# Lagging one half of TensorE by three products in the tail of two attention layers, with earlier splits and stores

## The chip, the cores and the metric

The kernel runs on one core of a Trainium2 chip. Its engines work at the same time, each from its own queue in order: TensorE (PE, with its weight loads shown apart as PEld), VectorE (DVE), ScalarE (ACT), GpSimd (POOL) and SyncE (SP), which here issues nearly all DMAs. An engine that needs another's result waits on a semaphore, and all that is queued behind the waiting instruction waits with it. The metric is the device time of one execution in microseconds (us); the time given for a kernel is the median of several runs.

## The reference, cut to what matters

Two attention layers over 2048 positions, width 576, 32 heads of 18. Their outputs stand side by side.

```
A: qkv = x @ wqkv; each position attends to 8 positions at distances 0, 2, ..., 14
   behind it (masked before the start); softmax over the 8; heads joined; @ wo
B: qkv = x @ wqkv; scores of all 2048 x 2048 pairs of each head, scaled by 18 ** -0.5;
   softmax over the keys; weighted sum of the values; heads joined; @ wo
out = concat(A, B) along the last axis          # 2048 x 1152, float32
```

All inputs are float32. The kernel keeps that precision on TensorE by splitting a number into a high part in TensorE's rounded format (F32R) and the low rest, and adding the products high x high, high x low, low x high.

## The kernel before, in words

**Projections.** The first part computes all queries, keys and values of both layers and stores them in DRAM (`dqk`, `dv`, `da`).

**Layer B.** The heads are taken in eight groups of four (`g`), the queries in four blocks of 512 (`b`), the keys in sixteen tiles of 128 (`kt`). One triple of these is a step; there are 512, and steps 448 to 511 are the last group, g = 7, with its blocks starting at steps 448, 464, 480 and 496. A step computes four score tiles, one per head, on TensorE (`score`, L271): heads 0 and 2 in the upper 64 rows of the array, heads 1 and 3 in the lower 64. ACT makes the exponential of each (L279), and a step later TensorE multiplies them with the values into the bank `po` (`weigh`, L744), where a column of ones gives the denominators too.

The maximum to be subtracted is found beforehand, for groups ahead of the one being weighed: TensorE computes the scores once more (L160), VectorE reduces them (L168). When a block's maxima are complete, `least` reduces them (L178), a step later `turn` transposes them on VectorE (L185), a step later `halve` splits them on POOL into a high and a low part (L103, L104), and two steps later in the last group `place` writes them by eight small DMAs into spare rows of the query tile `qs` (L197). The scores of that block then come out with the maximum already subtracted, so the first `score` of a block waits for these eight DMAs. In the last group the lead of the maxima has shrunk to a few steps.

**Order.** All engines get their instructions in the order in which the Python code makes them. What isn't part of a step's fixed pattern stands in an agenda: `later(n, f)` and `plan(start, ...)` put a piece of work at a step, and `due()` makes it at the end of that step, in the order in which it was put down. What a finished block needs is such a chain: `finish` copies `po` to `o`, the denominators go through DRAM and come back spread out (`den`, `drec`, `rec`, L787 to L790), POOL multiplies (L791), splits the result (L792, L793) and it is stored to `do`. For block (7,0), `finish` runs in step 464 and L791 is due 13 steps later.

**Output products of B.** The rows of `wo` for B are loaded into the buffer `y` (L858) by `load_wo`, in steps 455, 457, 459 and 461 for the four large chunks, and split six steps later on POOL into the room of an old group's queries and keys. After block b of the last group is done, `full(b)` makes eight sums, one for each of four position tiles `t` and two halves `h` of 288 columns; `sum_of` makes one. It puts the contraction's upper 64 rows and lower 64 rows on the two halves of the array, in two banks, by `beside`, which issues an upper and a lower product in turn (L1137). There are 14 products in each half, or 12 for the sums of block 3 that are made without the last group (`partial`). ACT then copies the upper bank into `y` (L1161) and VectorE adds the lower one (L1162). These banks come from a ring of three (`else`); scores have a ring of four.

While maxima are still to be computed, sums are placed inside a step (`inside`). When none are left, the loop is in its paired form (`paired`): scores of an even step, a sum, scores of an odd step, a sum, the weighing of both steps (16 products), and where many sums wait a third one behind it. From here to the end I call it the tail.

**The end.** When the last block has been weighed, `closing` normalises it in pieces, `first` and `some` make the remaining products (L1108), and `end` stores the four position tiles of block 3 (L1188). The results stand in the buffer `y`, of which there are four; `full` stores a position tile through `later(1, ...)` (L1201).

**DMA.** SP issues its DMAs in order, and an issue that waits for data holds up those behind it.

Of the kernel before, what the change touches and what calls it, by code (L numbers as in the profile page):

```python
# [10 lines left out]
AF = mybir.ActivationFunctionType  # L11
# [6 lines left out]
D = 576  # L18
# [4 lines left out]
NG = H // 4  # L23
# [9 lines left out]
STEPS = NB * NT  # L33
# [28 lines left out]
def two_attentions(ctx: ExitStack, tc, xa, wa, woa, xb, wb, wob, out):  # L62
# [19 lines left out]
    def bank(kind=None):  # L82
        r = rings[kind or ring]
        r.append(r.pop(0))
        return p_bank.tile([128, 512], F32, name=f"bank{r[-1]}")
# [24 lines left out]
    def later(n, f):  # L110
        agenda[step + n].append(f)
# [37 lines left out]
    def block(g, b):  # L149

        qs, ks = sets[g % 3]

        mx = maxes.tile([128, 2, 2, 4, NB, 2], F32, name="mx", bufs=3)
        left = 2 * PIECES

        def take(ps, r, t, k, p, part=None):

            at = slice(64 * r, 64 * r + 54)
            first, n = (0, 512) if part is None else (256 * part, 256)
            return nc.tensor.matmul(ps if part is None else ps[:, 256 * r : 256 * r + 256],  # L160
                                    qs[at, b, p, 128 * t : 128 * t + 128],
                                    ks[at, p, 512 * k + first : 512 * k + first + n], start=True, stop=True)

        def reduce(ps, r, t, k, p, part=None):

            nonlocal left
            at = mx[:, r, p, t, k] if part is None else mx[:, :, p, t, k, part]
            nc.vector.tensor_reduce(at, ps.rearrange("q (s n) -> q s n", s=2), axis=AX.X, op=ALU.max)  # L168

            settle()  # L170
            left -= 1
            if left == 0:
                owing.append(least)

        def least():
            m = least_rooms[n_least[0] % 2]
            n_least[0] += 1
            nc.vector.tensor_reduce(m[:, :16], mx.rearrange("q r p t k s -> q (r p t) (k s)"), axis=AX.X, op=ALU.max,  # L178
                                    negate=True)
            later(1, lambda: turn(m))  # L180

        def turn(m):

            raw = maxes.tile([128, 32], F32, name="mt", bufs=2)
            nc.vector.transpose(raw, m)  # L185
            later(1, lambda: halve(raw))

        def halve(raw):
            mh = maxes.tile([128, 32], F32R, name="mh", bufs=2)
            split_on(nc.gpsimd, mh, raw.bitcast(F32R), raw)  # L190
            later(2 if g == NG - 1 else 5, lambda: place(mh, raw))

        def place(*parts):
            placed.add((g, b))
            for k, t in enumerate(parts):
                for j in range(4):
                    load(ap(qs.bitcast(F32)[54 + k : 128 : 64, b, 0, 32 * j :], (128, 8), (1, 32)),  # L197
                         t.bitcast(F32)[32 * j : 32 * j + 16])

        return take, reduce  # L200
# [922 lines left out]
    def beside(kind, *both):  # L1123

        sums_ = [bank(k)[:, :288] for k in (kind, None)]
        turns = [[(sums_[r], *ab, i == 0, i == len(t) - 1) for i, ab in enumerate(t)] for r, t in enumerate(both)]
        pair = kind and sum(given) + 2 <= NG * NB * PIECES * 2
        if pair:

            for r in range(2):  # L1130
                turns[r].insert(6 + 4 * r, None)
        for i in range(max(map(len, turns))):
            for r in range(2):
                if i < len(turns[r]):
                    if turns[r][i]:
                        ps, a, b, start, stop = turns[r][i]
                        nc.tensor.matmul(ps, a, b, start=start, stop=stop)  # L1137
                    else:
                        maximum(r)()
        if pair:  # L1140

            rings["else"].append(rings["else"].pop(0))
        return sums_

    def sum_of(y, t, h, chunks, kind=None, stack=()):

        pos, cols = slice(128 * t, 128 * t + 128), slice(288 * h, 288 * h + 288)
        both = []
        for r in range(2):
            both.append([])  # L1150
            for c, (hi, lo) in enumerate(chunks):
                at = slice(64 * r, min(64 * r + 64, hi.shape[0]))
                whi, wlo = wo["b"][c]
                both[r] += [(a[at, pos], w[at, cols]) for a, w in ((hi, whi), (hi, wlo), (lo, whi))]
            at = slice(64 * r, 64 * r + 3 * DH)
            both[r] += [(a[at, pos], w[at, cols]) for a, w in zip(stack, wstack)]
        one, two = beside(kind, *both)
        if kind:
            nc.vector.tensor_copy(y, one)
        else:  # L1160
            nc.scalar.activation(y, one, AF.Copy)  # L1161
        nc.vector.tensor_add(y, two, y)  # L1162

    def first(t, b, h):
        sums[t, b, h] = bank()[:, :288]
# [19 lines left out]
    def end(t, b, new):  # L1185
        for h in range(2):
            half_end(t, b, h, new)
        load(out[512 * b + 128 * t : 512 * b + 128 * t + 128, D:], ys[t, b])  # L1188

    def full(b):  # L1190
        def half(t, h):
            if total - sum(given) > 4:
                inside.append(lambda: quarter(t, h, "scores"))
            else:
                waiting.append(lambda: quarter(t, h))

        def quarter(t, h, kind=None):
            if h == 0:
                ys[t, b] = work.tile([128, D], F32, name="y", bufs=4)
            if h == 1:  # L1200
                later(1, lambda: load(out[512 * b + 128 * t : 512 * b + 128 * t + 128, D:], ys[t, b]))  # L1201
            sum_of(ys[t, b][:, 288 * h : 288 * h + 288], t, h, olds[b], kind, stacks[b])

        return [(4 + 2 * t + h, lambda t=t, h=h: half(t, h)) for t in range(4) for h in range(2)]

# [9 lines left out]

    for k, src, start, chunks in (
        ("a", woa, 28, [[(0, 128 * c, 128)] for c in range(4)] + [[(64 * r, 512, 64) for r in range(2)]]),
        ("b", wob, STEPS * (NG - 1) + 7,
         [[(0, 126 * c, 126)] for c in range(4)] + [[(32 * i, 504 + DH * i, DH) for i in range(4)]]),
    ):  # L1220
        plan(start, [((4 if k == "a" else 2) * c if len(ch) < 4 else 421 - start, lambda k=k, src=src, c=c, ch=ch: load_wo(k, src, c, *ch))
                     for c, ch in enumerate(chunks)])
# [69 lines left out]
    while step < ALL:  # L1292
# [18 lines left out]
        whole = total - sum(given) > 1  # L1311
        parts = (bool(begun) or total - sum(given) > 3) and step not in copied

        ps = bank() if inside and whole else None


# [20 lines left out]
        for _ in range(1 if paired and step < ALL - 2 else len(waiting)):  # L1337
            if waiting:
                waiting.pop(0)()
        if ready and (kt % 2 == 0 or not paired):  # L1340
            weigh(ready.pop(0))
        ready.append((g, b, kt, es))
# [32 lines left out]
```

## Time and profile before

| | |
|---|---|
| median of 3 runs | 1598.83 us (1594.93 to 1600.14) |
| profiled execution, its own time | 1596.11 us |
| its span, first to last instruction | 1594.3 us |
| granted TensorE clock | 1.0 |
| busy: TensorE, VectorE, ACT, POOL | 99%, 86%, 76%, 61% |

How it is read: busy shares are averages over stages with different limits. The chain that ended last goes back from the last instruction, at each step to what released it. In a timeline row stand the start, the duration, the engine, the line, the operation, output and inputs by their names in the program, the shape, the count, and in brackets the idle time of that engine just before, with what ended it. In a row of stretches stand the stretch, its length, the busy time of PE, PEld, DVE, ACT and POOL with their instructions, the clock, the share of the DMA engines and GB/s. Matmuls are pipelined and their ends are modelled, so rows overlap.

### The profile page before, as it was taken

What the parts mean: (1) busy time and instruction counts of PE and PEld (TensorE: products, weight loads), DVE (VectorE), ACT (ScalarE), POOL (GpSimd) and SP (SyncE); (2) the same over time, 40 slices, a digit from 0 to 9 for tenths busy, and PEclk for the clock granted to TensorE, in tenths of its full rate; (3) what the DMA queues carried; (4) which work ended last, traced back from release to release, by engine and by line L of the source; (5) the groups of instructions that cost most, each with busy time, mean ns of one, the idle gap of its engine ahead of it and who ended that gap; (6) DMA issues with size and microseconds to landing.
All of it is one profiled execution on the core that took longest, in us unless ns stands there. A gap on an engine that the chain in (4) does not pass through costs nothing.

```text
span 1594.3 us, 34958 instructions
## 1 busy us (share of the span) xinstructions
PE 1582.1 (99%) x13274; PEld 963.1 (60%) x13274; DVE 1369.1 (86%) x2313; ACT 1216.3 (76%) x2436; POOL 964.9 (61%) x798
## 2 busy tenths in 40 slices
PE   9999999999999999999999999999999999999998
PEld 7999888999644445445445445445445444545676
DVE  5299999999999999999989999999999999988622
ACT  6423441121699999999999999999999999998565
POOL 2405742211166996995896896896897898781000
PEclk9999999999999999999999999999999999999999
DMA  8938854532312352245226324422621331154311
GB/s 251 229 124 211 274 157 128 160 101 71 74 34 70 68 138 71 75 117 111 74 76 131 87 92 116 107 80 59 141 93 37 91 104 50 46 173 132 130 62 61
DMA packets 188025, 175.66 MB, mean 110 GB/s; under 512 B 119416, under 2 KB 133240, under 8 KB 186128
## 3 DMA queue, kind: packets, MB, share of 16 engines
q1 hardware_dynamic: 182992, 161.88, 36.7%
q0 software_dynamic: 4032, 10.63, 3.3%
q8 instruction: 104, 1.70, 0.5%
q10 hardware_dynamic: 832, 0.92, 0.2%
q14 instruction: 65, 0.53, 0.1%
HBM read 98.77 MB, written 73.47 MB: 108 GB/s over the span
## 4 chain that ended last, share of the span: by engine, by line
PE 94%; DVE 3%; POOL 1%; ACT 1%; issue 1%; DMA 0%; SPq 0%; POOLq 0%; DVEq 0%
PE po L744 30%; PE bank L271 19%; PE bank L160 17%; PE bank L366 16%; PE bank L303 5%; PE bank L1137 4%; PE bank L1264 4%; DVE mx L168 2%; POOL xlo L414 1%; PE bank L518 0%; ACT e L279 0%; SPq L197 0%; DMA out<-y 0%; DVE wlo L414 0%; DVE as L942 0%
## 5 line engine op out<-in xcount | busy, mean ns | idle before, releaser
L168 DVE TENSOR_REDUCE mx<-bank 128x2 f32<-128x512 f32 x2048 | 1278.8, 682 | 118.5 <-PE bank L160 89.1
L279 ACT ACTIVATE e<-bank 128x512 f32<-128x512 f32 x2048 | 1048.3, 606 | 62.3 <-PE bank L271 56.0
L160 PE MATMUL bank<-ks,qs 54*128 54x512 f32 (+1 forms) x2464 | 790.9, 381 | 2.1 <-DVE mx L168 1.2
L160 PEld LDWEIGHTS bank<-ks,qs 54*128 54x128 f32 x2464 | 403.0, 184 | 382.9 <-DVE mx L168 332.7
L271 PE MATMUL bank<-qs,ks 56*128 56x512 f32 x2048 | 592.5, 425 | 2.7 <-DMA qs<-mt 2.3
L744 PE MATMUL po<-e,v 128*19 128x512 f32 x4096 | 531.6, 599 | 0.1
L271 PEld LDWEIGHTS bank<-qs,ks 56*128 56x128 f32 x2048 | 308.8, 184 | 34.8 <-ACT e L279 25.1
L925 POOL TENSOR_TENSOR pr<-aq,akv 128x1024 f32<-128x1024 f32 x72 | 158.4, 2202 | 15.9 <-DMA akv<-da 13.0
L967 POOL TENSOR_TENSOR pr<-lg,akv 128x1024 f32<-128x1024 f32 x72 | 158.3, 2199 | 0.5
L744 PEld LDWEIGHTS po<-e,v 128*19 128x19 f32 x4096 | 73.7, 97 | 138.0 <-issue 132.1
L929 POOL TENSOR_TENSOR pr<-pr 128x1024 f32<-128x1024 f32 x64 | 152.7, 2386 | 5.0
L694 ACT ACTIVATE ohi<-bank 128x512 f32<-128x512 f32 (+1 forms) x56 | 30.4, 595 | 150.5 <-issue 107.7
L366 PE MATMUL bank<-xhi,ahi 64*128 64x512 f32 (+1 forms) x448 | 114.2, 387 | 0.0
L366 PE MATMUL bank<-xhi,alo 64*128 64x512 f32 (+1 forms) x448 | 112.1, 387 | 0.0
L366 PE MATMUL bank<-xlo,ahi 64*128 64x512 f32 (+1 forms) x448 | 111.1, 388 | 0.1
L1264 PE MATMUL bank<-wohi,at 64*128 64x288 f32 x480 | 103.2, 304 | 0.0
L968 POOL TENSOR_TENSOR pr<-pr 128x512 f32<-128x512 f32 x72 | 92.4, 1283 | 5.6
L1264 PEld LDWEIGHTS bank<-wohi,at 64*128 64x128 f32 x480 | 74.7, 184 | 27.6 <-ACT e L279 23.8
L414 POOL TENSOR_TENSOR alo<-raw,ahi 128x512 fp32r<-128x512 f32 (+1 forms) x14 | 17.6, 1255 | 121.6 <-ACT ahi L413 93.1
L506 POOL TENSOR_TENSOR olo<-olo,ohi 128x512 fp32r<-128x512 f32 x36 | 46.1, 1293 | 69.4 <-ACT ohi L505 59.4
L1264 PE MATMUL bank<-wolo,at 64*128 64x288 f32 x240 | 70.9, 295 | 0.0
L366 PEld LDWEIGHTS bank<-xhi,ahi 64*128 64x128 f32 (+1 forms) x448 | 64.8, 182 | 3.3
(200 smaller groups left out, 1795.6 us busy)
## 6 DMA issues: line engine op xcount, KB each, us to landing
do<-n SPq DMA_DIRECT2D x30, 512.0 KB
da<-ohi SPq DMA_DIRECT2D x52, 256.0 KB
akv<-da SPq DMA_DIRECT2D x64, 175.5 KB
out<-y SPq DMA_DIRECT2D x32, 288.0 KB
qs<-dqk SPq DMA_DIRECT2D x30, 288.0 KB
ks<-dqk SPq DMA_DIRECT2D x30, 288.0 KB
at<-dao SPq DMA_DIRECT2D x60, 128.0 KB
rec<-drec SPq DMA_DIRECT2D x29, 256.0 KB
```

Of the source, the lines that this page charges most:

```text
L160: return nc.tensor.matmul(ps if part is None else ps[:, 256 * r : 256 * r + 256], qs[at, b, p, 128 * t : 128 * t + 128], ks[at, p, 512 * k ...
L168: nc.vector.tensor_reduce(at, ps.rearrange("q (s n) -> q s n", s=2), axis=AX.X, op=ALU.max)
L271: nc.tensor.matmul(ps, ks[at, p, 128 * kt : 128 * kt + 128], qs[at, b, p], start=True, stop=True)
L279: nc.scalar.activation(e, ps, AF.Exp, scale=SCALE)
L303: nc.tensor.matmul(ps, a, b, start=c == i == 0, stop=c == 4 and i == 1)
L366: nc.tensor.matmul(ps, a, b, start=start, stop=stop)
L744: nc.tensor.matmul(po[32 * i : 32 * i + 19], vs[g][:, kt, 19 * i : 19 * i + 19], es[i], start=kt == 0, stop=kt == NT - 1)
L925: nc.gpsimd.tensor_mul(pr, ap(st["q"][:, 2 * c], (SUB, 2), (0, W), (1, SUB)), window(st["k"], c))
L929: nc.gpsimd.tensor_add(st["pr"], st["pr"], pr)
L967: nc.gpsimd.tensor_mul(at, ap(st["lg"], (0, 2), (SUB, W), (1, SUB)), window(st["v"], c))
L968: nc.gpsimd.tensor_add(at[:, :, :4], at[:, :, :4], at[:, :, 4:])
L1264: return nc.tensor.matmul(ps, a, b, start=r == k == 0, stop=r == 1 and k == len(both[1]) - 1)
```

## The change

There are five edits.

1. In `turn`, a block of the last group is split (`halve`) in the same step as it is transposed; `place` keeps its distance of two steps to the split.
2. `sum_of`, outside the `inside` form, no longer calls `beside`. It issues a product of the upper half, puts the matching one of the lower half into a queue `behind`, and issues from that queue until at most three are left in the paired form, none otherwise. So in the tail the lower half's last three products of one sum go beside the first three of the next, past scores and weighing. The upper bank is copied when the last upper product is issued, the lower one added when the last lower product is. The queue is emptied at the start of a step that has maxima or other inserted work, and in steps 510 and 511 after their sums.
3. `full` stores a position tile as soon as the addition of its second half is issued, no longer through the agenda one step later; the `inside` form still does.
4. `end` stores the last position tile (t = 3) in two halves of 288 columns, each as it is ready.
5. The four large weight chunks of B are loaded in steps 458 to 464 instead of 455 to 461; their splits move with them.

```diff
             nc.vector.transpose(raw, m)
-            later(1, lambda: halve(raw))
+            if g == NG - 1:
+                halve(raw)
+            else:
+                later(1, lambda: halve(raw))
...
-    def sum_of(y, t, h, chunks, kind=None, stack=()):
+    def sum_of(y, t, h, chunks, kind=None, stack=(), done=lambda: None):
...
-        one, two = beside(kind, *both)
         if kind:
+            one, two = beside(kind, *both)
             nc.vector.tensor_copy(y, one)
-        else:
-            nc.scalar.activation(y, one, AF.Copy)
-        nc.vector.tensor_add(y, two, y)
+            nc.vector.tensor_add(y, two, y)
+            done()
+            return
+        sums_ = [None, None]
+
+        def piece(r, i):
+            if i == 0:
+                sums_[r] = bank()[:, :288]
+            last = i == len(both[r]) - 1
+            nc.tensor.matmul(sums_[r], *both[r][i], start=i == 0, stop=last)
+            if last and r == 0:
+                nc.scalar.activation(y, sums_[0], AF.Copy)
+            elif last:
+                nc.vector.tensor_add(y, sums_[1], y)
+                done()
+
+        for i in range(len(both[0])):
+            piece(0, i)
+            behind.append(lambda i=i: piece(1, i))
+            catch_up(3 if paired else 0)
+
+    behind = deque()
+
+    def catch_up(n=0):
+
+        while len(behind) > n:
+            behind.popleft()()
...
     def end(t, b, new):
         for h in range(2):
             half_end(t, b, h, new)
-        load(out[512 * b + 128 * t : 512 * b + 128 * t + 128, D:], ys[t, b])
+            if t == 3:
+                load(out[512 * b + 128 * t : 512 * b + 128 * t + 128, D + 288 * h : D + 288 * h + 288],
+                     ys[t, b][:, 288 * h : 288 * h + 288])
+        if t < 3:
+            load(out[512 * b + 128 * t : 512 * b + 128 * t + 128, D:], ys[t, b])
...
-            if h == 1:
-                later(1, lambda: load(out[512 * b + 128 * t : 512 * b + 128 * t + 128, D:], ys[t, b]))
-            sum_of(ys[t, b][:, 288 * h : 288 * h + 288], t, h, olds[b], kind, stacks[b])
+            y = ys[t, b]
+
+            def done():
+                if h == 1:
+                    store = lambda: load(out[512 * b + 128 * t : 512 * b + 128 * t + 128, D:], y)
+                    later(1, store) if kind else store()
+
+            sum_of(y[:, 288 * h : 288 * h + 288], t, h, olds[b], kind, stacks[b], done)
...
-        ("b", wob, STEPS * (NG - 1) + 7,
+        ("b", wob, STEPS * (NG - 1) + 10,
...
+        if whole or parts or outside or inside:
+            catch_up()
         ps = bank() if inside and whole else None
...
         for _ in range(1 if paired and step < ALL - 2 else len(waiting)):
             if waiting:
                 waiting.pop(0)()
+        if step >= ALL - 2:
+            catch_up()
```

## The prediction

> **What bounds the kernel now.** I read the page first, then the chain that ended last, then, wherever the chain leaves TensorE, the timelines of the engines there.
>
> ```profile
> span 1594.3 us, 34958 instructions
> PE 1582.1 (99%) x13274; PEld 963.1 (60%) x13274; DVE 1369.1 (86%) x2313; ACT 1216.3 (76%) x2436; POOL 964.9 (61%) x798
> PE 94%; DVE 3%; POOL 1%; ACT 1%; issue 1%; DMA 0%; SPq 0%; POOLq 0%; DVEq 0%
> L168 DVE TENSOR_REDUCE mx<-bank 128x2 f32<-128x512 f32 x2048 | 1278.8, 682 | 118.5 <-PE bank L160 89.1
> ```
>
> TensorE is on 94% of the chain and VectorE's maxima fill most of the rest of the span. The change adds and removes no product, exponential or reduction; it moves waits. So only what TensorE waits for in the last group and after it can be won or lost: three places, A, B and D, and a row of small ones, C.
>
> **A. The maxima of block (7,2), split one step earlier.** TensorE's longest wait in the last group, with the chain into it (start, duration in us):
>
> ```profile
> 1462.37 0.47 PE L271 MATMUL bank<-qs,ks 56*128 56x512 f32 x1 [2.34 <-DMA qs<-mt]
> 1460.49 1.53 DMA qs<-mt
> 1456.42 2.30 SPq L197 DMA_DIRECT2D qs<-mh  x4
> 1458.82 2.17 SPq L197 DMA_DIRECT2D qs<-mt  x4
> 1451.25 0.20 DVE L185 STREAM_TRANSPOSE mt<-m 128x32 f32<-128x32 f32 x1
> 1454.96 1.29 POOL L791 TENSOR_TENSOR o<-o,rec 128x512 f32<-128x512 f32 x1 [17.99 <-DVE mx L168]
> 1456.19 0.20 POOL L103 CAST mh<-mt 128x32 fp32r<-128x32 f32 x1
> 1444.68 0.56 SPq L790 DMA_DIRECT2D rec<-drec  x1
> ```
>
> The transposed maxima are there at 1451.45, but their split (L103 and the subtraction after it) stands on POOL behind L791, which waits until 1454.96. The releaser named there, a reduction, is not what L791 reads; it reads rec, whose load was issued at 1444.68. In the code the turn of this block falls in step 476, the split in 477, and L791 is in 477 too, written into the agenda at step 464 and so ahead of it. Split in 476, it stands before L791. POOL has been idle for 17.99 us, so the split begins at 1451.45. The eight stores into the query rows follow 0.23 later (1456.42 - 1456.19), are issued over 4.07 (1460.49 - 1456.42) and land after 1.53: 1457.3, plus 0.35 from landing (1462.02) to product: 1457.6. TensorE came to the wait at 1462.37 - 2.34 = 1460.03. So the whole wait goes: -2.34. On SP the stores pass no DMA (the queue is empty from 1445.2 to 1456.4); POOL's L791 waits for rec either way and loses nothing. Late next is whatever step 480 needs; VectorE idles there too, for want of TensorE. Bounds: 0, if the stores land as slowly as those of block (7,1) in B, where the eight took 9.3 instead of 4.5; -2.34. I take -2.34, because the congestion ends by 1454.96, when rec is there.
>
> **B. B's output weights loaded three steps later.** Block (7,1) had the two first weight chunks ahead of it on SP; block (7,0) had not:
>
> ```profile
> 1408.26 1.80 SPq L858 DMA_DIRECT2D y<-wob  x2
> 1412.57 3.38 SPq L197 DMA_DIRECT2D qs<-mh  x4
> 1416.87 4.98 SPq L197 DMA_DIRECT2D qs<-mt  x4
> 1373.62 2.31 SPq L197 DMA_DIRECT2D qs<-mh  x4
> 1376.03 2.15 SPq L197 DMA_DIRECT2D qs<-mt  x4
> 1421.43 1.89 DVE L168 TENSOR_REDUCE mx<-bank 128x2 f32<-128x512 f32 x3 [0.16 <-PE bank L160]
> 1423.89 1.29 DVE L168 TENSOR_REDUCE mx<-bank 128x2 f32<-128x512 f32 x2 [0.58 <-PE bank L160]
> 1423.24 0.39 PE bank L271
> ```
>
> The eight stores stretch to 1421.85, and the first product of step 464 starts at 1423.24 instead of about 1422.8; VectorE idles 0.58 there against 0.16 a step before. That is 0.42 of stall. With chunks at steps 458 to 464 all eight stores go ahead of them: -0.42 (bounds 0 and -0.58). The chunks now pass, on SP, the store of n, drec, rec and the two stores of the A parts, or stand between them; on POOL their splits mix with L791 to L793 of block (6,3).
>
> ```profile
> 1435.01 0.91 SPq L997 DMA_DIRECT2D at<-dao  x2
> 1445.73 0.40 PE L1264 MATMUL bank<-wohi,at 64*128 64x288 f32 x1
> 1422.00:1426.00 4.00, 3.64 (x30) 1.20 (x22) 3.42 (x7) 3.52 (x8) 3.72 (x4) 1.00 0.79 228
> ```
>
> Two more chunks behind the stores are 2 x 290 KB, at the 228 GB/s of that stretch 2.5 us. The next loads TensorE needs are issued by 1435.9 and used at 1445.73, and POOL is idle for 18 us after this block: cost 0 (bounds 0 and +2.5, should everything behind shift into the use). The weights themselves are first used in step 486, by the code, 22 steps after the last of these loads.
>
> **C. The lower half three products behind.** A sum of output columns runs in two halves of the array, each into its own bank, out of three. In program order upper and lower products alternate before and after the change; only which lower product goes with which upper one differs. One sum that follows scores, with ACT beside it, and the sums as the chain shows them (first and last of the eight that follow the odd step's scores and hold 28 products; first and last of three that follow scores after the weighing, where nothing waits):
>
> ```profile
> 1558.52 0.59 PE L1137 MATMUL bank<-qs,wohi 64*128 64x288 f32 x2
> 1558.72 0.53 PE L1137 MATMUL bank<-ks,wohi 64*128 64x288 f32 x2
> 1556.23 2.07 ACT L279 ACTIVATE e<-bank 128x512 f32<-128x512 f32 x4 [2.02 <-PE bank L271]
> 1558.25 0.41 ACT L1161 ACTIVATE y<-bank 128x288 f32<-128x288 f32 x1
> 1516.38 2.04 PE bank L1137 x26
> 1572.79 2.03 PE bank L1137 x26
> 1556.36 1.85 PE bank L1137 x28
> 1570.33 1.86 PE bank L1137 x27
> 1504.21 2.16 PE bank L1137 x26
> 1549.21 2.01 PE bank L1137 x25
> 1522.81 1.90 PE bank L1137 x24
> ```
>
> The lower half's first product needs the bank that the sum before used above, and ACT copies it out only after four exponentials (1558.25 to 1558.66). The sum starts at 1558.52, its second products at 1558.72, just after the copy. Three products later, about 0.4 us, the copy is long done, so the wait goes: 2.04 - 1.85 = 0.19, eight times, 1.52. The first sum in the new order, at 1504.21, has the same wait (2.16 - 1.85 = 0.31) and that at 1549.21 too (2.01 - 1.85 = 0.16). The four sums of 24 products (1522.81 is one) are slow by some 0.27, 24 products being 24/28 of 1.85 = 1.59 and the row 1.90; I count them 0, because the scores behind them wait for ACT's fourth exponential, which does not come earlier. Paid once: before the last score step three lower products run alone, 3 x 0.13 = 0.40 (14 pairs in 1.85). Sum: 1.52 + 0.31 + 0.16 - 0.40 = 1.59 won. Bounds: 0.40 lost, if something else takes the place of every wait; 2.7 won, if the 24s give 0.27 each as well. I take -1.59, nearest to the rows of sums that wait for nothing.
>
> **D. The closing stores.**
>
> ```profile
> 1588.99 0.29 PE L1108 MATMUL bank<-qs,n 128*128 128x288 f32 x1
> 1587.42 2.48 DMA out<-y
> 1590.01 0.41 ACT L1181 ACTIVATE y<-bank 128x288 f32<-128x288 f32 x1 [2.78 <-DMA out<-y]
> 1590.03 0.46 DVE L1183 COPY y<-bank 128x288 f32<-128x288 f32 x1 [1.04 <-DMA out<-y]
> 1590.93 0.42 SPq L1201 DMA_DIRECT2D out<-y  x1
> ```
>
> The last product ends at 1589.28, but the last two copies wait until 1590.0 for a store to land: the first closing store, issued at 1587.42 and landed 2.48 later. Its buffer is taken again because one of the four y buffers is still held by the last sum of part C, whose store (L1201) the agenda issues only after the closing, last of all, at 1590.93. Issued at once, as changed, that store is away before the last scores are weighed and its buffer is free. The copies then start 0.7 earlier (1590.03 - 1589.32), the last store goes out at 1590.55 - 0.7 = 1589.85 instead of 1590.93: 1.08. It is also half as large, for which I take another 0.2 of its 2.48: -1.3. Bounds: -0.38 (only the queue place, 1590.93 - 1590.55, if the buffer is still waited for) and -1.5. One store more on SP costs 0.33 while SP waits for the copies: 0. By the Trainium skill, DMA: Bandwidth & Descriptors, section Anatomy of one DMA, about 2.0 us of a transfer are fixed, and by that half the bytes save little: -1.1. The row of 2.48 agrees with most being fixed; nothing else hangs on this.
>
> **Sum.** 2.34 + 0.42 + 1.59 + 1.3 = 5.65 us. The profiled execution took 1596.11 (span 1594.3 and 1.8 around it), so 1590.5 by its own time. It lies 2.7 below the median shown, 1598.83; from the median it is 1593.2, 0.35% less. A measurement of this kernel tells about 0.3%, 4.8 us, from no change.
>
> **The rivals.** R1: the placement of (7,2) is late in another way, its stores as slow as in B: 1451.7 + 9.3 of issue + 1.0 to land + 0.35 = 1462.4, as before, and 3.3 are left: 1595.5. Against it: rec has landed by 1454.96. R2: ACT sets the tail. Its four exponentials take 2.07 and the next scores need their banks, so the waits only change places; C becomes +0.40 and the sum 3.66: 1595.2. For it: the second copy of exponentials follows the copy without idle. Against: ACT idles 2.02 per pair of steps. By the Trainium skill, TensorE: Matmul & The Clock Gate, section on the array of 32x32 sub-arrays, ACT's queue is strictly in order; this favours R2, and the rows (copy behind exponentials) agree. R3: the change doesn't do what it says, the order of the agenda keeps L791 ahead and the stores late: 1598.8. R4, on the other side: a lower bank is now held over the weighing and given back only in the next sum, so VectorE's addition into y comes late, and the sum after it waits for that bank. It has 10 products and the scores, 1.3 + 0.47 us, and the addition takes 0.46:
>
> ```profile
> 1558.69 0.46 DVE L1162 TENSOR_TENSOR y<-bank,y 128x288 f32<-128x288 f32 x1 [4.00 <-PE bank L271]
> ```
>
> so it must be 1.3 us late to begin to cost, and 0.24 more on each of the 24 sums to eat the 5.65; at 0.6 on each it is +14.4 - 5.65: 1607.6. VectorE idles 4.00 ahead of such an addition, which speaks against it.
>
> **How the numbers follow.** Forecast 64%, R1 8%, R2 10%, R3 6%, R4 12%, more than its row bears, for losses in the order of instructions that a trace of before cannot show. The forecast's own range is 1589 to 1596.5: all upper bounds together are 2.34 + 0.58 + 2.7 + 1.5 = 7.1, and the runs spread by 2.6 about their middle. The range given, 1589 to 1598.3, takes in R1 and R2. Of the 64%, 53 lie beyond 4.8 us and 11 within; of R1 and R2 3 lie beyond. Faster 0.56, same 0.32, slower 0.12.
>
> **What would show it.** A: no wait of L271 on the query rows, and L103 ahead of L791 on POOL. B: eight stores in about 5 us, and no 0.58 on VectorE near step 464. C: the eight sums at 1.85, three lower products alone before the last scores. D: no wait of L1181 on a store; SP ends with half a y. Wrong would make it: a new wait of L271 or L1264 on a DMA between 1420 and 1480, or waits of L1137 on VectorE.

## The result, and the profile after

The changed kernel takes 1593.0 us (median of 15 runs, 1590.73 to 1594.35), the kernel before 1597.42 us (median of 15 runs on the same chips): the ratio is 0.9974, with a 95% interval of 0.9966 to 0.9982, so 2.9 to 5.4 us less. One execution of the kernel before took 2439.07 us, and the ratio is taken without it. The profiled execution took 1593.83 us. Some rows of the page of the changed kernel (line numbers after the change are higher by 3 to 40: `score` is L274, `weigh` L747, the tail's sums L1172, the closing copies L1208 and L1210):

```profile
span 1592.0 us, 34962 instructions
PE 1581.6 (99%) x13274; PEld 973.7 (61%) x13274; DVE 1371.2 (86%) x2313; ACT 1215.9 (76%) x2436; POOL 965.1 (61%) x798
L274 PE MATMUL bank<-qs,ks 56*128 56x512 f32 x2048 | 593.1, 425 | 0.0
```

The products are as many as before, and the score products (last row) no longer idle anywhere; before it was 2.7 us, 2.3 of them for a DMA. The span is only 2.3 us shorter than in the profile of before, 1592.0 against 1594.3, because this execution lost time elsewhere: the first exponential of layer B starts at 416.20 us, 2.45 later than in the profile of before (413.75). The projections ahead of it are the same code. Over the fourteen profiled executions of this study that start lies between 413.61 and 416.56, whatever was edited, so a span by itself cannot judge a change of 4 us here. What can is a table of stages. Each number runs from the start of one instruction to the start of another in the timeline: from the first exponential of step 448 to that of 464, and so on to step 511; from there to the last product; from the last product to the last copy into `y`; and from there to the end of the span.

| kernel | 448 to 464 | 464 to 480 | 480 to 496 | 496 to 511 | 511 to last product | to last copy | to the end | sum |
|---|---|---|---|---|---|---|---|---|
| before | 35.05 | 39.14 | 59.69 | 56.84 | 9.47 | 1.03 | 4.29 | 205.51 |
| changed | 34.65 | 36.74 | 59.32 | 56.01 | 9.59 | 0.33 | 4.12 | 200.75 |
| e1_split_late | 34.63 | 38.31 | 59.31 | 56.03 | 9.58 | 0.33 | 4.12 | 202.31 |
| e2_chunks_early | 34.65 | 36.74 | 59.26 | 56.01 | 9.60 | 0.33 | 4.35 | 200.93 |
| g11_neither | 34.68 | 37.74 | 59.22 | 55.98 | 9.60 | 0.33 | 4.13 | 201.67 |
| h12_again | 34.63 | 38.57 | 59.69 | 56.84 | 9.47 | 1.05 | 4.28 | 204.53 |
| e3_no_lag | 34.64 | 36.74 | 59.73 | 56.84 | 9.47 | 0.33 | 4.11 | 201.86 |
| f8_lag1 | 34.64 | 36.75 | 59.51 | 55.93 | 9.47 | 0.33 | 4.14 | 200.77 |
| f6_copy_dve | 34.65 | 36.74 | 59.28 | 55.98 | 9.58 | 0.33 | 3.99 | 200.55 |
| f7_dve_no_lag | 34.62 | 36.70 | 59.70 | 57.22 | 9.54 | 0.33 | 3.97 | 202.08 |
| e4_one_store | 34.64 | 36.70 | 59.30 | 56.01 | 9.58 | 0.33 | 3.75 | 200.32 |
| f5_store_late | 34.63 | 36.72 | 59.33 | 56.01 | 9.60 | 1.00 | 4.84 | 202.14 |
| g9_order | 34.64 | 36.74 | 58.74 | 55.44 | 9.59 | 0.33 | 3.96 | 199.43 |
| g10_all | 34.65 | 36.74 | 58.77 | 55.34 | 9.57 | 0.33 | 3.57 | 198.98 |

Where no transfer is waited for, a stage repeats to within some 0.1 us, so the table resolves what the medians cannot. The last stage holds the landing of a store: in the nine kernels that end with the same two half stores it lies between 3.96 and 4.35. Before against changed, the change won 0.40 and 2.40 in the two stages of B and A, 0.37 + 0.83 - 0.12 = 1.08 in C's three, and 0.70 + 0.17 = 0.87 in D's two: 4.76 in all, the 2.3 of the spans and the 2.45 lost ahead of layer B.

**A, around step 480.** POOL and then SP in the timeline of the changed kernel; in brackets the idle time before and what ended it:

```profile
1453.57 0.21 POOL L103 CAST mh<-mt 128x32 fp32r<-128x32 f32 x1 [13.18 <-DVE mt L185]
1456.38 1.29 POOL L794 TENSOR_TENSOR o<-o,rec 128x512 f32<-128x512 f32 x1 [2.27 <-DMA rec<-drec]
1453.80 2.30 SPq L200 DMA_DIRECT2D qs<-mh  x4
1456.20 2.17 SPq L200 DMA_DIRECT2D qs<-mt  x4
```

The split now starts as soon as the transposed maxima are there and stands ahead of the multiplication that waits for the reciprocals. The eight stores start 2.6 us before that multiplication, and no score waits: TensorE waits for nothing from 1400 to 1480 us.

**B, around step 464.** SP in the timeline of the changed kernel, and under it the first score of step 464 in the timeline of the kernel before:

```profile
1414.72 2.33 SPq L200 DMA_DIRECT2D qs<-mh  x4
1417.15 3.53 SPq L200 DMA_DIRECT2D qs<-mt  x4
1420.73 0.43 SPq L861 DMA_DIRECT2D y<-wob  x1
```

```profile
1423.24 0.46 PE L271 MATMUL bank<-qs,ks 56*128 56x512 f32 x1 [0.36 <-ACT e L279]
```

The eight stores of block (7,1) now go ahead of the chunks and are issued over 5.96 us instead of 9.28. The row of before names an exponential as what ended its wait, but in the trace TensorE's queue stood until 1422.93 at its check for the last of these stores, which landed at 1422.89. The trace of before also shows what spread the stores: the transfers take eight semaphores in turn, and an issue waits until the transfer eight issues earlier has landed. The last two stores were issued at 1420.68 and 1421.33, 0.01 to 0.02 us after the two chunks had landed (1420.66 and 1421.32).

**C, the tail.** Pieces of the chain that ended last (start, duration, engine, line, number of products on the chain; some of a sum's run beside it, so a sum of 28 can stand as x24): the first sum that lags, a pair of steps with three sums, part of one with two, and the lone products at the end. Under them the sum of 24 and the scores behind it in the chain of the kernel before.

```profile
1503.92 1.85 PE bank L1172 x24
...
1510.87 2.06 PE bank L1172 x24
1512.93 0.47 PE bank L274 x4
1513.40 1.59 PE bank L1172 x24
1514.99 0.80 PE bank L274 x4
1515.79 1.95 PE bank L1172 x27
1517.74 1.84 PE po L747 x16
...
1557.00 0.59 PE bank L274 x4
1557.59 1.89 PE bank L1172 x27
...
1577.54 0.13 PE bank L274
1577.66 0.13 PE bank L1172
1577.80 0.61 PE bank L274 x3
```

```profile
1514.00 1.87 PE bank L1137 x24
1515.87 0.51 PE bank L271 x4
```

Sums of 28 behind the odd step's scores, which took 2.03 to 2.04, take 1.95 where a sum of 24 products is ahead and 1.89 elsewhere. The sums of 24 between two scores (1513.40) fell from 1.87 to 1.59, and the scores behind them rose from 0.51 to 0.80: that part of the wait only moved.

**D, the end.** VectorE's last copy and SP's last issues:

```profile
1587.92 0.46 DVE L1210 COPY y<-bank 128x288 f32<-128x288 f32 x1 [0.34 <-PE bank L1111]
1586.03 1.92 SPq L1219 DMA_DIRECT2D out<-y  x3
1588.04 0.90 SPq L1216 DMA_DIRECT2D out<-y  x2
```

The copy follows the last product and no store.

### The profile page after: what moved, and what is told of

It is laid out like the page before. It is cut to its first block, busy times and chain, and to the rows that moved or that the text cites. A ratio compares the mean times of both kernels' runs of the same rounds, so it can differ in the third digit from the quotient of the medians.

```text
span 1592.0 us, 34962 instructions
## 1 busy us (share of the span) xinstructions
PE 1581.6 (99%) x13274; PEld 973.7 (61%) x13274; DVE 1371.2 (86%) x2313; ACT 1215.9 (76%) x2436; POOL 965.1 (61%) x798
## 4 chain that ended last, share of the span: by engine, by line
PE 92%; DMA 2%; DVE 2%; POOL 1%; issue 1%; ACT 1%; SPq 0%; POOLq 0%; DVEq 0%; ACTq 0%
PE po L747 30%; PE bank L274 19%; PE bank L160 17%; PE bank L369 13%; PE bank L306 5%; PE bank L1300 4%; PE bank L1172 3%; DVE mx L168 2%; DMA raw<-xa 1%; POOL xlo L417 1%; POOL olo L509 0%; DMA dqk<-olo 0%; PE bank L1140 0%; ACT e L282 0%; PE bank L1111 0%
## 5 line engine op out<-in xcount | busy, mean ns | idle before, releaser
L274 PE MATMUL bank<-qs,ks 56*128 56x512 f32 x2048 | 593.1, 425 | 0.0
L747 PE MATMUL po<-e,v 128*19 128x512 f32 x4096 | 531.6, 598 | 0.1
L274 PEld LDWEIGHTS bank<-qs,ks 56*128 56x128 f32 x2048 | 309.0, 184 | 32.5 <-ACT e L282 26.0
L747 PEld LDWEIGHTS po<-e,v 128*19 128x19 f32 x4096 | 73.7, 97 | 138.0 <-issue 132.4
L369 PE MATMUL bank<-xlo,ahi 64*128 64x512 f32 (+1 forms) x448 | 116.6, 388 | 0.1
L369 PE MATMUL bank<-xhi,alo 64*128 64x512 f32 (+1 forms) x448 | 115.3, 387 | 0.0
L103 POOL CAST mh<-mt 128x32 fp32r<-128x32 f32 x32 | 6.7, 208 | 113.9 <-DVE mt L185 113.9
```

Of the source, the lines that this page charges most:

```text
L274: nc.tensor.matmul(ps, ks[at, p, 128 * kt : 128 * kt + 128], qs[at, b, p], start=True, stop=True)
L747: nc.tensor.matmul(po[32 * i : 32 * i + 19], vs[g][:, kt, 19 * i : 19 * i + 19], es[i], start=kt == 0, stop=kt == NT - 1)
```

## The experiments

All edits are made to the changed kernel, except in the one that runs the kernel before again.

**A and B: which of the two moves takes which wait away?**

```diff
-            if g == NG - 1:
-                halve(raw)
-            else:
-                later(1, lambda: halve(raw))
+            later(1, lambda: halve(raw))
```

> The changed kernel with the split of the last group's maxima back in the step after the transposition; all else as changed. Theory: the split stands behind the multiplication that waits for rec again, the first scores of block (7,2) wait some 2.4 us for the query rows, and the time is about 2.4 us above the changed kernel, 2 us below the kernel before. Rival (the wait is gone because the weight chunks moved, not because of the split): no such wait, time as changed.

1593.7 us, ratio to before 0.9986 (0.9976 to 0.9996). The wait is back, at 1.56 where some 2.4 was expected, with the split behind the multiplication again (score, then POOL):

```profile
1461.91 0.46 PE L271 MATMUL bank<-qs,ks 56*128 56x512 f32 x1 [1.56 <-DMA qs<-mt]
1454.49 1.29 POOL L791 TENSOR_TENSOR o<-o,rec 128x512 f32<-128x512 f32 x1 [14.74 <-DMA rec<-drec]
1455.73 0.20 POOL L103 CAST mh<-mt 128x32 fp32r<-128x32 f32 x1
```

```diff
-        ("b", wob, STEPS * (NG - 1) + 10,
+        ("b", wob, STEPS * (NG - 1) + 7,
```

> The changed kernel with the four weight chunks of B back at steps 455 to 461. Theory: the stores of block (7,1) are issued over some 9 us instead of 7, the first scores of step 464 wait about 0.4 us again, time 0.4 us above the changed kernel; the place of block (7,2) is untouched. Rival (the split one step earlier gets the stores out in time as it does for (7,2)): no wait in step 464, no difference.

1592.46 us, 0.9977 (0.9968 to 0.9986). The rival held. Neither wait is there; with the chunks at their old steps the table's first two stages are those of the changed kernel. With the split a step earlier, `place` too is written a step earlier, and SP gets only one chunk ahead of the stores of block (7,1) and the second behind them:

```profile
1409.59 1.10 SPq L861 DMA_DIRECT2D y<-wob  x1
1413.02 2.34 SPq L200 DMA_DIRECT2D qs<-mh  x4
1416.29 4.35 SPq L200 DMA_DIRECT2D qs<-mt  x4
1420.68 0.42 SPq L861 DMA_DIRECT2D y<-wob  x1
```

After these two it seemed that either move alone removes the stall of step 464, and that the later chunks make the late split 0.8 cheaper. Both readings compare single executions, so I undid both moves together.

> The changed kernel with both moves ahead of the tail undone: the maxima of block (7,2) split a step later and B's weight chunks three steps earlier, as before. Theory (either move alone takes the stall of step 464 away, the split alone or together with the chunks takes that of step 480): both stalls are back, 448 to 464 takes 35.0 us and 464 to 480 takes 39.1, as before, while the stages after 480 keep what they won. Rival (the stalls of before hung on something else that the change moved, the lag or the stores): 34.65 and less than 38.5.

1592.86 us, 0.9979 (0.9968 to 0.9989). My theory fell: with both moves undone there was no stall at step 464 (34.68), and that of step 480 was 0.98, the smallest of all, as the rival had it. But up to step 480 the traces of this kernel and of the kernel before hold the same instructions in the same order on ACT, VectorE, POOL and SP, and as many on TensorE, so no later edit can be the cause. So I ran the kernel before once more.

> The kernel before once more, nothing edited: a second profiled execution of it. With both moves undone the stalls were 0.97 and none where the kernel before had 2.34 and 0.42, and up to step 496 the two issue the same instructions in the same order. Theory (the stall of step 480 hangs on when the reciprocals' load lands, which over the executions so far lay between 29.3 and 31.1 us after step 464's first exponential, whatever was moved; the 0.42 of step 464 came of one execution's slow transfers): 464 to 480 takes between 37.3 and 39.2 us, 448 to 464 between 34.6 and 35.05, each most likely not at the upper end; the stages after 480 come out as in the first profile within 0.1 (59.7, 56.8, 9.5, 1.0, 4.3). Rival (something in the tail's edits reaches back to these steps): 39.1 and 35.05 again, within 0.1.

1597.42 us, 1.0002 (0.999 to 1.0013). The stages from 480 on repeat those of the first profile to within 0.02. The two ahead do not: 34.63 and 38.57. From the timeline of this second execution, VectorE near step 464, the score of step 480, and SP and POOL ahead of it; under them the score, SP and POOL with both moves undone:

```profile
1422.59 3.92 DVE L168 TENSOR_REDUCE mx<-bank 128x2 f32<-128x512 f32 x6 [0.16 <-PE bank L160]
1462.56 0.46 PE L271 MATMUL bank<-qs,ks 56*128 56x512 f32 x1 [1.79 <-DMA qs<-mt]
1444.68 0.57 SPq L790 DMA_DIRECT2D rec<-drec  x1
1455.13 1.29 POOL L791 TENSOR_TENSOR o<-o,rec 128x512 f32<-128x512 f32 x1 [18.13 <-DVE mx L168]
```

```profile
1460.39 0.47 PE L271 MATMUL bank<-qs,ks 56*128 56x512 f32 x1 [0.98 <-DMA qs<-mt]
1442.74 0.57 SPq L790 DMA_DIRECT2D rec<-drec  x1
1452.96 1.29 POOL L791 TENSOR_TENSOR o<-o,rec 128x512 f32<-128x512 f32 x1 [18.04 <-DMA rec<-drec]
```

The multiplication starts some 10.3 us after the load of the reciprocals is issued in both (9.4 to 10.8 over the fourteen executions). That load stands behind four large loads and a store that SP issued just before, and they land one after the other: in the first profile the loads at 1445.08, 1447.24, 1448.75 and 1450.86, the store at 1452.16, the reciprocals at 1454.80. What differs most is when that row of transfers comes, measured against TensorE's work: of the 0.84 us between these two executions 0.61 is the time of the issue. The multiplication starts between 29.3 and 31.1 us after the first exponential of step 464 in the fourteen executions, with no relation to the edits, and where the split is late the wait follows it: 2.34, 1.79, 1.56 and 0.98 at 31.10, 30.53, 30.27 and 29.69. So the late split costs 1.0 to 2.4 us by the execution (stage 464 to 480 at 39.14, 38.57, 38.31 and 37.74 with it, 36.70 to 36.75 in all ten without), on average 1.7. The 0.42 of step 464 was in one execution out of three with the old order. That the earlier split cures the wait is shown; that the later chunks win anything is not.

**C: what does the lag hide?**

```diff
-            catch_up(3 if paired else 0)
+            catch_up(0 if paired else 0)
```

> The changed kernel with the lower half never behind: the queue of lower products is emptied after every upper one. Theory: the odd steps' sums of 28 products take 2.04 us on the chain again instead of 1.89 to 1.95, the sums of 24 take 1.9 instead of 1.6 while the scores behind them take 0.5 instead of 0.8, and the lone products before the last scores (0.24 us) go; from step 496 to the last product about 1.1 us is lost against the changed kernel. Rival (the lag gains nothing, ACT only moves the waits): 0.2 us won.

1593.62 us, 0.9985 (0.9975 to 0.9995). The three stages of the tail are those of the kernel before to within 0.04, the other stages those of the changed one: C is the lag alone, 0.41 + 0.83 - 0.12 = 1.12. The size is the one expected, though 0.41 of it lies ahead of step 496.

```diff
-                nc.scalar.activation(y, sums_[0], AF.Copy)
+                (nc.vector.tensor_copy(y, sums_[0]) if paired else nc.scalar.activation(y, sums_[0], AF.Copy))
```

> The changed kernel with the upper bank of the paired sums copied into y by VectorE instead of ScalarE; lower half three products behind as in the changed kernel. Theory (what still holds the tail is ScalarE's queue, in which the copy stands behind four exponentials and then delays the next ones): the scores behind the sums of 24 products go from 0.80 back to about 0.5 us, the sums of the stretches with three sums from 1.95 to about 1.87, and from step 496 to step 511 it takes 54.5 to 55 us instead of 56.01. Rival 1: the scores wait for ScalarE's exponentials whatever else it does (four take 2.07 us against about 1.85 for a sum): 56.0, no change. Rival 2: VectorE now has two operations of about 0.45 us per sum and its maxima and additions come late: over 56.5, with waits of the sums on VectorE.

1592.24 us, 0.9972 (0.9961 to 0.9984). The theory fell, rival 1 held: 55.98. The chain around the same sums, and then ACT's timeline beside them:

```profile
1512.30 1.59 PE bank L1172 x24
1513.89 0.79 PE bank L274 x4
1514.68 1.96 PE bank L1172 x27
```

```profile
1512.16 4.05 ACT L282 ACTIVATE e<-bank 128x512 f32<-128x512 f32 x8 [3.97 <-PE bank L274]
```

ACT has nothing to do now but eight exponentials, which follow one another without a gap, 0.51 us each, and the scores between still take 0.79. ACT's other work was not the cause; what is left is the four exponentials of the step before, and the other order of the sums further down bears this out.

The same edit, and the halves level (`catch_up(0)`):

> The changed kernel with both: the paired sums' copy on VectorE and the two halves level, as before the change. Theory (the lag is only a way round the copy's place behind the exponentials): with the copy on VectorE, which is idle when the sum ends, the bank comes free at once and the lag has nothing left to hide: 496 to 511 takes 54.5 to 55.8 us against 56.84 with the halves level and the copy on ScalarE, and the three products alone ahead of the last scores are not paid (0.12). Rival (the wait is that of the bank itself, so that any copy of 0.41 us between two sums is seen): 56.6 to 57 us, and only the lag helps.

1593.58 us, 0.9978 (0.9966 to 0.999): 57.22 from 496 to 511, worse than with ACT's copy (56.84). The rival held, a little beyond its 56.6 to 57. A sum in the chain of this kernel, VectorE's copy ahead of it in its timeline, and then the same place in the timeline of the kernel before, the last four products of a sum:

```profile
1557.28 2.08 PE bank L1172 x26
```

```profile
1556.72 0.46 DVE L1174 COPY y<-bank 128x288 f32<-128x288 f32 x1 [3.43 <-PE bank L1172]
```

```profile
1557.78 0.43 PE L1137 MATMUL bank<-qs,at 54*128 54x288 f32 x4
```

Before the change the sum ends at 1558.21, and ACT's copy, quoted in the prediction, starts at 1558.25. In the paired form of that kernel all copies but one (0.12) start within 0.06 us of the end of their sum, so the copy was not late. On VectorE it starts with the end of the sum as well and takes 0.46 instead of 0.41, and the sum behind it takes 2.08 instead of 2.03: the 0.05 of the longer copy appears whole in the sum. What the lag hides is the length of the copy itself, which the scores between two sums do not quite cover: the next sum's first product starts 0.31 after the end of this one (1558.52, also quoted there), the copy ends 0.45 after it (1558.66).

```diff
-            catch_up(3 if paired else 0)
+            catch_up(1 if paired else 0)
```

> The changed kernel with the lower half one product behind instead of three. Theory (the wait is the rest of the copy, about 0.2 us a sum, and one product more gives 0.13 of it): 496 to 511 takes 56.0 to 56.4 us, the first stretch from 480 to 496 59.3 to 59.5, and of the 0.12 paid before the last scores two thirds come back. Rival (the copy's delay varies and only the whole 0.4 covers it): 56.6 to 56.85, nearly as with no lag.

1592.25 us, 0.9972 (0.9963 to 0.9982). The rival fell, and the lag of one did better than the theory, which had 56.0 to 56.4: one product is enough from 496 on (55.93), nothing is paid at the end (9.47 as before), and only the stage with the longer wait of the first sums loses 0.19. The sum of the row, 200.77, is that of three products.

**Where the rest of C's waits sits.** In each pair of steps with three sums, one of 24 products now comes right behind the weighing and one of 28 between the two scores:

```diff
-        waiting.append(lambda: sum_of(y, t, h, olds[b]))
+        short.append(lambda: sum_of(y, t, h, olds[b]))
+        waiting.append(short[-1])
...
+    def take(short, any_, wanted=False):
+        at = 0
+        if wanted:
+            at = next((i for i, f in enumerate(waiting) if f in short), 0)
+        elif not any_:
+            at = next((i for i, f in enumerate(waiting) if f not in short), 0)
+        return waiting.pop(at)
...
-                waiting.pop(0)()
+                take(short, not (paired and kt % 2 == 0))()
...
-            waiting.pop(0)()
+            take(short, True, paired)()
```

> The changed kernel with the sums in the tail in another order: in a pair of steps with three sums, the one of 24 products comes right after the weighing and one of 28 stands between the two scores, instead of the other way round. Theory (the score steps are held by ScalarE's four exponentials of the step before, some 0.5 us each: about 2.55 us from the first of four scores to the last of the next four, and only a sum of 28 in between is long enough to cover that): four such pairs go from 2.06 + 0.47 + 1.59 + 0.80 + 1.95 = 6.87 to about 1.79 + 0.47 + 1.86 + 0.60 + 1.90 = 6.62 us, so 496 to 511 takes about 55.0 us instead of 56.01, everything else as in the changed kernel. Rival (the 0.80 and the 1.95 belong to the sums of 24 themselves, to their copies or to their data): the loss moves with them, 55.8 to 56.1.

1591.0 us, 0.9961 (0.9947 to 0.9975). The chain through the first such pair:

```profile
1508.11 1.78 PE bank L1173 x24
1509.90 0.47 PE bank L274 x4
1510.36 1.87 PE bank L1173 x28
1512.23 0.59 PE bank L274 x4
1512.82 1.90 PE bank L1173 x27
```

6.61 us against 6.87, as expected for the pair. My place for it was wrong: the first of the four pairs and the first sum of the second lie ahead of step 496, so 0.58 comes in the stage 480 to 496 and 0.57 in 496 to 511, 1.15 in all where 1.0 was expected.

**D: the buffer and the half store.** The last paired sum's store goes back into the agenda, so behind the closing:

```diff
-                    later(1, store) if kind else store()
+                    later(1, store)
```

> The changed kernel with the last paired sum's store again written into the agenda, so issued after the closing. Theory (the buffer held by this store is what the closing copies waited for): the two copies after the last product wait again for the first closing store, from the last product's start to the last copy 1.03 us as before instead of 0.33, and this store goes out last of all, behind the half store, so the span ends some 0.9 us later by its own stages (rows of the changed kernel and of the kernel before); nothing else moves. Rival (with the half store cut off in another place a buffer is free in time anyway): the copies stay at 0.33 and only the queue place is lost, at most 0.4 us.

1593.72 us, 0.9981 (0.9972 to 0.9991). The theory held for the copies (1.00), and it was too small for the store: 0.67 + 0.72 = 1.39 where 0.9 was expected. In the timeline of SP the store now stands behind two half stores and the wait ahead of them:

```profile
1583.63 1.92 SPq L1219 DMA_DIRECT2D out<-y  x3
1586.62 0.81 SPq L1216 DMA_DIRECT2D out<-y  x2
1587.47 0.45 SPq L1235 DMA_DIRECT2D out<-y  x1
```

```diff
-            if t == 3:
...
-        if t < 3:
+        if True:
             load(out[512 * b + 128 * t : 512 * b + 128 * t + 128, D:], ys[t, b])
```

> The changed kernel with the last position tile stored in one piece, as before the change. Theory: the change of the end won 0.7 us by the free buffer and the rest of what was expected was lost in SP's last checks: the last store's semaphore is the first of eight that SP looks at in order, so the seven others (0.06 each) come after it lands. With one store fewer the last semaphore is the last in that order again: the time from the last copy to the end of the span is 0.3 to 0.4 us shorter than as changed (about 3.7 instead of 4.1 us). Rival (half a store lands earlier): 0.2 us longer.

1592.72 us, 0.9978 (0.9969 to 0.9987). One store instead of two halves ends 0.37 sooner, 3.75 after the last copy instead of 4.12. The last half store lands 2.15 us after its issue, the whole one 2.30 after. By the Trainium skill, DMA: Bandwidth & Descriptors, section Anatomy of one DMA, about 2.0 us of a transfer issued by GpSimd do not scale with its size; these are issued by SP, and the traces agree in kind: the last store lands 2.01 to 2.40 us after its issue where it is a half (nine executions), 2.11 to 2.45 where it is whole (five). The half store lands hardly sooner after the start of the last copy than the whole one, 2.76 against 2.83 us. The rest comes after landing: SP closes the program with a row of checks on semaphores, started 0.06 us apart and always in the same order; eight of these semaphores are those that the transfers take in turn. The checks of the changed kernel and of this one, with the operations that follow them (count, duration in ns, first and last start):

```profile
L1411 SPq EVENT_SEMAPHORE  x12: 17/28/28, 1589.0 to 1592.0; - x12
```

```profile
L1408 SPq EVENT_SEMAPHORE  x12: 17/28/28, 1586.4 to 1589.2; - x12
```

With one transfer more, the last one's semaphore is the first of the eight to be looked at; the other seven checks follow its landing at 1590.68, and the span ends 1.36 us after it. Here, as in the kernel before, the last transfer's semaphore is looked at last, and the span ends 0.93 after the landing. That is 0.43, less the 0.07 of the earlier landing: 0.36, the 0.37 of the rounded stages. No other execution differs from this: the span ends 1.35 to 1.36 after the last landing in the ten that have the last transfer on the first of the eight, 0.93 in the four that have it on the last.

**All together.** The order of g9_order, the lower half two products behind, the last tile stored whole:

> The changed kernel with three things together: the order of sums just named, the lower half two products behind instead of three, and the last block's closing part stored whole as before. Theory: the three add up, each in its own stage: 55.0 us from 496 to 511 (order), 59.3 to 59.45 from 480 to 496 and 9.5 from 511 to the last product (two products behind cover the 0.17 of the copy, and less is paid at the end), and 3.75 from the last copy to the end of the span (one transfer fewer): 199.2 us from step 448 on against 200.75 for the changed kernel. Rival (two products are too few for the longer wait of the first sums, or the gains share a stage): 199.8 or more.

1591.61 us, 0.9966 (0.9952 to 0.9979). The stages add up to 198.98 us where 199.2 was expected, 1.77 less than the changed kernel and the least of all. The order's part is split over two stages as in g9_order (58.77 and 55.34), and the whole store's is in the last (3.57). Two products behind instead of three won next to nothing: 9.57 to the last product where 9.5 was expected, and of the 0.45 us gained on g9_order 0.39 lies in the last stage. The medians of this kernel and of g9_order, 1591.61 and 1591.0, do not tell the two apart. Their intervals end at 0.9979 and 0.9975, that of the changed kernel begins at 0.9966, so that they are faster than the changed kernel is shown by the stages and not by the times.

## Why the prediction was right or wrong

**The time.** 1593.2 was forecast and 1593.0 came, but the measured gain of 0.26% (0.18 to 0.34), clear of zero as it is, lies below the 0.3% from which the prediction spoke of a change, so what it held likeliest, faster, did not come. The agreement is partly luck: the sum of 5.65 was taken from a median of three runs, 1598.83, which fifteen runs put at 1597.42. Against the measured 2.9 to 5.4 us the sum was too large. With the terms as the runs show them it is 1.7 (A) + 0.1 (B) + 1.1 (C) + 0.9 (D) = 3.8.

**A, 2.34: the mechanism right, the size that of one execution.** The split stands ahead of the multiplication, the stores pass, nothing waits, as said. But the wait is as long as the reciprocals are late, and 2.34 was the longest of the four executions with the late split, whose average is 1.7. I took the number of one profile for a property of the kernel.

**B, 0.42: wrong.** The step "with chunks at steps 458 to 464 all eight stores go ahead of them: -0.42" failed. The order on SP is as predicted, and the stall of that one profile did come from the stores. But it was in one of three executions with the old order, and the earlier split alone already moves the second chunk behind the stores. The later chunks leave more room for stores that run late; that this ever shortens the path beside the earlier split is not shown.

**C, 1.59: 1.08 to 1.12.** That the lag hides the wait was right, and the two single sums came out as predicted (2.16 to 1.85, and 2.01 to 1.86). Two sizes were off. The eight sums won 0.09 (four of them) and 0.14 instead of 0.19, 0.92 instead of 1.52. In the first four, 0.05 goes with the sum of 24 ahead of them, as the other order shows (1.90); the remaining 0.04 to 0.05 of each sum I have not traced. The lone products cost about 0.2 instead of 0.40, by the run with one product of lag (0.08 and 0.12 in the last two stages): in the chain only one of the three shows, the others ran beside scores. Counting the sums of 24 as nothing was right, and for the reason given: the scores behind them wait for the fourth exponential. There R2 holds, and for the rest of C it does not. One reason was wrong though the number stood: "ACT copies it out only after four exponentials" is no delay, since the copy starts 0.04 us after the sum ends. By the Trainium skill, TensorE: Matmul & The Clock Gate, section on the array of 32x32 sub-arrays, ACT's queue is in order. The trace agrees, the copy at 1558.25 comes behind the four exponentials from 1556.23 on, but here it costs nothing, as taking the copy off ACT won nothing (55.98 against 56.01).

**D, 1.3: 0.87.** The 0.7 of the buffer came to the digit, and the undone store brought it back. Of the other 0.6 only 0.17 came. The last store does land 0.6 sooner, 2.76 instead of 3.36 us after the start of the last copy, but 0.43 of it goes back into SP's closing checks, which were not in the sum at all. So the half store, which was to save 0.2, costs 0.37, and with the last tile stored whole the end wins 0.70 + 0.54 = 1.24.

**The rivals.** R1 and R3 did not come: POOL and SP are in the order predicted and the stores are fast. R4 did not come: no sum in the chain of the changed kernel is more than 0.01 longer than before.

## What to carry to other kernels

A wait for a transfer that one profile shows has a spread of its own: before it is priced, look at what the transfer queues behind and, where there is a second execution, compare the same stage there. When a copy stands between two uses of a bank, look first at whether it starts late or is merely long: a copy that starts on time gains nothing from another engine, but a lag of one product hid its length here. Where an engine's pieces of work differ in length, the long ones belong where another engine needs the time, which won 1.15 us here without an instruction more or less.

## What was not expected of the hardware

The same instructions ahead of layer B took up to 3 us more or less from execution to execution (413.61 to 416.56 us), where the fifteen times of the changed kernel are spread over 3.6, while the stages from step 480 on repeated to 0.02 us between two executions of the kernel before. What makes the difference ahead of layer B is not shown. The closing checks of SP are the other: which semaphore the last transfer happens to take was worth 0.43 us at the end of these kernels.
